# A cached-attention decode kernel on one core: K and V by the slab of a head instead of by quarters, and the softmax cut into pieces

## The chip, the cores and the metric

The kernel runs on one core of a Trainium2 chip. The metric is device time in microseconds (us). Where several runs are compared, all were in the fast state; times are medians, and a ratio is the mean time of one kernel's fast runs over the mean of the other's fast runs of the same rounds, so it is not quite the ratio of the medians quoted. Engines: PE is TensorE (matmuls), DVE is VectorE, ACT is ScalarE, POOL is GpSimd, SP issues the DMAs.

## The reference, cut to what matters

```python
# B=8 sequences, one new token each; 32 query heads share 8 K/V heads; 8192 cached positions of 128
h = layernorm(x) * (1 + ca) + sa
q = h @ wq
scores = einsum(q, k_cache) * 128 ** -0.5
p = softmax(scores);  o = einsum(p, v_cache)
x = x + ga * (o @ wo)
... # a small MLP on x follows
```

K and V together are 268.4 MB, and each byte is used once. Everything else is small.

## The kernel before

The caches are read by units: a quarter of one head's K or V, 512 KB. In each of the 128 partitions a unit is one contiguous run of 16 x 128 bf16 values, 4 KB. The ring has 20 slots, each freed by itself:

```python
def k_units(b): return [("K", b, g, k) for k in range(UPS) for g in range(HKV)]   # UPS = 4, HKV = 8
...
def emit_dma(n):
    s = n % NSLOT                                   # NSLOT = 20
    if n - NSLOT >= 0:
        waits.append(("pe", unit_done[n - NSLOT]))
    step("sp", lambda e: e.dma_start(kv_ring[:, s, :]..., kv_src(u)), waits, ("kv%d" % s, 16))
```

A K unit is transposed on PE, copied out of psA, the PSUM tile that the transposes write, half by DVE (0.69 us for 128x1024) and half by ACT (1.01 us; together the evacuation), then multiplied with the queries (QK). A V unit is multiplied with the probabilities P (PV). PE takes six K units of the next batch ahead (LAG = 6), then K and V by turns. The softmax of a batch runs when its last scores are there:

```python
gq = POOL partition_all_reduce(max)
d2 = cstep("dve", ... tensor_tensor(sview, sview, gb, ALU.subtract), [("gp", gq)])     # 2048 columns
EXP[b] = cstep("act", ... activation(PT_sb, S_sb, ACTF.Exp), w)                        # 2048 columns
...
def emit_sums(b):                                    # before the first PV of b
    sm = mm_group(... ones_h x PT_sb, four matmuls of 512 columns ...)
    RED_done[b] = tensor_reduce;  d_r = reciprocal
    SC_done[b] = cstep("dve", ... tensor_tensor(ptv, ptv, rsb, ALU.mult), ...)         # P scaled, 2048 columns
```

What stood behind such a block in the program of DVE or ACT waited for it: in the prediction's timeline DVE's copies of 179.91 us start as the 2.29 us subtraction of 177.70 us ends, and ACT's of 181.84 us as the 1.91 us exponential of 180.03 us ends, though their transposes were done at 177.2 us.

## Time and profile before

| | before |
|---|---|
| time, median of 15 runs | 756.69 us (753.67 to 758.26) |
| profiled span | 754.0 us |
| PE busy | 76% |
| read from HBM | 283.66 MB |
| plateau of the stream | 407 to 409 GB/s |
| last V unit taken up | 735.2 us |

The busy shares don't tell the bound here; the row of GB/s by slices does (the profile's page cuts the span into 40 equal slices), and what ended the waits of PE tells why that row has dips. The lines are in the prediction.

### The profile page before, as it was taken

The page shows a single profiled execution, that of the slowest core. Times are in us where ns is not written, and L with a number is a line of the kernel's source. Part 1 is how long each engine was busy: PE and PEld are TensorE (multiplying, and loading weights), DVE is VectorE, ACT ScalarE, POOL GpSimd, SP SyncE. Part 2 cuts the span into 40 slices and gives each one's busy share as a digit, 9 for nine tenths or more (in the row PEclk, how much of TensorE's full clock was granted, in tenths as well). Part 3 has the DMA queues.
Part 4 walks back from the last instruction along what each step waited for, and adds up shares of the span by engine and source line. Part 5 has one row for each costly group of instructions (what it writes and reads, how often), then busy time and mean ns, then how long its engine had stood idle before and what let it go on. Part 6 is the DMA issues. An engine that isn't in the chain of part 4 may idle for free.

```text
span 754.0 us, 27966 instructions
## 1 busy us (share of the span) xinstructions
PE 570.1 (76%) x12812; PEld 553.4 (73%) x12820; DVE 252.9 (34%) x379; ACT 298.4 (40%) x314; POOL 4.6 (1%) x17
## 2 busy tenths in 40 slices
PE   3588578876888859885788867798688857988354
PEld 3588578876788859885788867798588846978254
DVE  0244432323433252233323334332532333323302
ACT  2266534443444344452443433443444423534102
POOL 0000000000000000000000000000000000000000
PEclk9999777785887667696687767866687876877555
DMA  8999999999999999999899998999989998999980
GB/s 347 409 408 402 363 403 407 407 407 408 408 406 407 408 395 365 409 407 408 324 378 406 407 408 283 403 407 407 401 315 409 407 408 314 367 408 408 387 320 2
DMA packets 81444, 285.48 MB, mean 379 GB/s; under 512 B 8344, under 2 KB 14256, under 8 KB 80816
## 3 DMA queue, kind: packets, MB, share of 16 engines
q1 hardware_dynamic: 81328, 283.70, 96.3%
q8 instruction: 102, 1.67, 0.9%
q14 instruction: 14, 0.11, 0.0%
HBM read 283.66 MB, written 0.01 MB: 376 GB/s over the span
## 4 chain that ended last, share of the span: by engine, by line
PE 68%; issue 18%; DVE 7%; DMA 3%; ACT 2%; SPq 0%; POOL 0%; ACTq 0%; DVEq 0%; POOLq 0%
PE psA L256 41%; PE psS L293 13%; PE psO L380 13%; DMA W<-in_A_wq_dram 3%; DVE PT_sb L364 2%; DVE S_sb L341 2%; ACT kt_ring L276 2%; PE psM L150 1%; DVE tmax L333 1%; DVE tmax L325 1%; DVE ssum L360 1%; ACT S_sb L309 1%; POOL gmax L337 0%; DVE rs_all L361 0%; SPq L405 0%
## 5 line engine op out<-in xcount | busy, mean ns | idle before, releaser
L276 ACT COPY kt_ring<-psA 128x1024 bf16<-128x1024 bf16 x256 | 258.2, 1012 | 344.6 <-PE psA L256 344.6
L256 PE MATMUL psA<-ident,kv_ring 128*128 128x128 bf16 x4096 | 365.6, 260 | 35.0 <-issue 24.7
L256 PEld LDWEIGHTS psA<-ident,kv_ring 128*128 128x128 bf16 x4096 | 314.7, 119 | 38.2 <-issue 37.9
L275 DVE COPY kt_ring<-psA 128x1024 bf16<-128x1024 bf16 x256 | 176.2, 691 | 404.6 <-PE psA L256 404.5
L293 PE MATMUL psS<-qT_sb,kt_ring 128*128 128x4 bf16 x4096 | 147.3, 166 | 59.8 <-ACT kt_ring L276 40.9
L293 PEld LDWEIGHTS psS<-qT_sb,kt_ring 128*128 128x128 bf16 x4096 | 140.7, 101 | 63.0 <-issue 59.5
L380 PE MATMUL psO<-PT_sb,kv_ring 128*128 128x4 bf16 x4096 | 136.1, 167 | 63.1 <-issue 33.6
L380 PEld LDWEIGHTS psO<-PT_sb,kv_ring 128*128 128x128 bf16 x4096 | 121.6, 100 | 70.6 <-issue 69.4
L345 ACT ACTIVATE PT_sb<-S_sb 128x2048 bf16<-128x2048 f32 x8 | 15.3, 1909 | 38.4 <-DVE S_sb L341 38.4
L309 ACT COPY S_sb<-psS 128x512 f32<-128x512 f32 x32 | 18.9, 592 | 5.5 <-PE psS L293 5.5
L341 DVE TENSOR_TENSOR S_sb<-S_sb,gmax 128x2048 f32<-128x2048 f32 x8 | 18.3, 2292 | 4.5 <-POOL gmax L337 4.5
L364 DVE TENSOR_TENSOR PT_sb<-PT_sb,rs_all 128x2048 bf16<-128x2048 bf16 x8 | 18.3, 2292 | 0.3
L325 DVE TENSOR_TENSOR tmax<-tmax,S_sb 128x512 f32<-128x512 f32 x16 | 11.1, 692 | 20.7 <-ACT S_sb L309 20.7
L150 PE MATMUL psM<-PT_sb,ones_h 128*128 128x512 bf16 x24 | 7.1, 410 | 8.5 <-ACT PT_sb L345 7.9
L494 ACT CAST oT_sb<-psO 128x256 bf16<-128x256 f32 x1 | 0.4, 372 | 28.4 <-PE psO L380 28.4
L150 PEld LDWEIGHTS psM<-PT_sb,ones_h 128*128 128x128 bf16 x32 | 2.6, 100 | 9.8 <-ACT PT_sb L345 7.6
L501 DVE TENSOR_TENSOR tC<-psS,modT 128x32 f32<-128x32 f32 x1 | 0.2, 191 | 27.0 <-PE psS L150 27.0
L150 PE MATMUL psM<-hT_bf,W 128*128 128x8 bf16 x128 | 3.6, 168 | 6.3 <-DMA W<-in_A_wq_dram 6.3
L360 DVE TENSOR_REDUCE ssum<-psM 128x32 f32<-128x512 f32 x8 | 5.5, 692 | 8.2 <-PE psM L150 8.2
L150 PEld LDWEIGHTS psM<-hT_bf,W 128*128 128x128 bf16 x128 | 3.5, 104 | 6.4 <-issue 6.4
L322 DVE TENSOR_TENSOR tmax<-S_sb 128x512 f32<-128x512 f32 x8 | 5.5, 692 | 7.3 <-ACT S_sb L309 7.3
L333 DVE TENSOR_TENSOR tmax<-tmax 128x256 f32<-128x256 f32 (+2 forms) x24 | 7.5, 314 | 0.8
(69 smaller groups left out, 49.7 us busy)
## 6 DMA issues: line engine op xcount, KB each, us to landing
kv_ring<-in_A_k_cache_dram SPq DMA_DIRECT2D x256, 512.0 KB, 13.0
kv_ring<-in_A_v_cache_dram SPq DMA_DIRECT2D x256, 512.0 KB, 12.5
W<-in_A_wq_dram SPq DMA_DIRECT2D x4, 1024.0 KB, 17.3
W<-in_A_wo_dram SPq DMA_DIRECT2D x1, 4096.0 KB, 25.2
W<-in_B_w_dram SPq DMA_DIRECT2D x2, 1792.0 KB, 22.6
W<-in_w_mod_dram SPq DMA_DIRECT2D x1, 3072.0 KB, 11.9
x_sb<-in_A_x_dram SPq DMA_DIRECT2D x1, 8.0 KB
c_sb<-in_c_dram SPq DMA_DIRECT2D x1, 8.0 KB
```

The source lines that it names most:

```text
L150: lambda e, o_=o_, l_=l_, r_=r_, i=i: e.matmul(o_, lhsT=l_, rhs=r_, start=(i == 0), stop=(i == n - 1)),
L256: lambda e, tl=tl: e.transpose(psA_bf[:, base + tl * P: base + (tl + 1) * P], kv_ring[:, slot, tl * DH:(tl + 1) * DH], ident[:, :],),
L275: dv = cstep("dve", lambda e: e.tensor_copy(kt_ring[:, ks, 0: 8 * P], psA_bf[:, base: base + 8 * P]), w)
L276: av = cstep("act", lambda e: e.copy(kt_ring[:, ks, 8 * P: 16 * P], psA_bf[:, base + 8 * P: base + 16 * P]), w)
L293: lambda e, tl=tl: e.matmul(psS[:, half + tl * HQ + REP * g: half + tl * HQ + REP * (g + 1)], lhsT=kt_ring[:, ks, tl * P:(tl + 1) * P], rh ...
L309: sv = cstep("act", lambda e: e.copy(S_sb[:, b % 2, k * 512:(k + 1) * 512], psS[:, half: half + 512]), w)
L325: RUNMAX[b] = cstep("dve", lambda e: e.tensor_tensor(tm, tm, Q, ALU.max), [("dve", RUNMAX[b]), ("act", sv)])
L333: d = cstep("dve", lambda e, hlf=hlf: e.tensor_tensor(tm[:, 0:hlf], tm[:, 0:hlf], tm[:, hlf:2 * hlf], ALU.max), [("dve", d)])
L341: d2 = cstep("dve", lambda e: e.tensor_tensor(sview, sview, gb, ALU.subtract), [("gp", gq)])
L345: EXP[b] = cstep("act", lambda e: e.activation(PT_sb[:, par, :], S_sb[:, par, :], ACTF.Exp), w)
L364: SC_done[b] = cstep("dve", lambda e: e.tensor_tensor(ptv, ptv, rsb, ALU.mult), [("dve", d_r)])
L380: lambda e, tl=tl, t=t: e.matmul(o_cols, lhsT=kv_ring[:, slot, tl * DH:(tl + 1) * DH], rhs=PT_sb[:, par, t * HQ + REP * g: t * HQ + REP * ...
```

## The change

It is meant to stream K and V in longer contiguous pieces and to keep the softmax out of the way of PE. (1) One transfer is a whole head's K or V, 2 MB, 16 KB in each partition; the ring has the same 10 MB as five slab slots, and a slot is refilled when its last unit is done. For that, K goes by head. (2) Subtraction and exponential are cut into four pieces each, placed one or two at a time behind the evacuations of the next batch's K units. (3) P is no longer scaled: a DVE reduction and one small matmul give the sums among the late V units, and the reciprocals multiply the output at the very end. (4) PE takes eight K units ahead instead of six.

```diff
-    NSLOT = 20
+    NSS = 5
+    NSLOT = NSS * UPS
-    LAG = 6
+    LAG = 8
...
-            return [("K", b, g, k) for k in range(UPS) for g in range(HKV)]
+            return [("K", b, g, k) for g in range(HKV) for k in range(UPS)]
...
+            if key not in slab_slot:            # key = (K or V, b, g)
+                if ss_hist[ss]:
+                    prev = ss_hist[ss][-1]
+                    waits.append(("pe", max(unit_done[m] for m in slab_units[prev])))
+                step("sp", lambda e: e.dma_start(kv_ring[:, ss * UPS:(ss + 1) * UPS, :]..., slab_src(*key)), waits, ("kv%d" % ss, 16))
...
-            d2 = cstep("dve", lambda e: e.tensor_tensor(sview, sview, gb, ALU.subtract), [("gp", gq)])
-            EXP[b] = cstep("act", lambda e: e.activation(PT_sb[:, par, :], S_sb[:, par, :], ACTF.Exp), w)
+            for j in range(NPH):
+                todo.append(lambda j=j: emit_sub(b, j))     # 512 columns
+                todo.append(lambda j=j: emit_exp(b, j))     # 512 columns
...
-            SC_done[b] = cstep("dve", lambda e: e.tensor_tensor(ptv, ptv, rsb, ALU.mult), [("dve", d_r)])
...
+                if g == HKV - 2 and k == 0:
+                    emit_reduce(b)
+                if g == HKV - 1 and k == 0:
+                    emit_sums(b)
...
-        d_oT = cstep("act", lambda e: e.copy(oT_sb[:, :], psO[:, 0:B * HQ]), [("pe", PVL)])
+        d_oT = cstep("dve", lambda e: e.tensor_tensor(oT_sb[:, :], psO[:, 0:B * HQ], rs_all[:, :], ALU.mult), ...)
```

## The prediction

> **What bounds the kernel now.** I read the page's slices first, then the busy time by stretch, then the waits, then the timeline around one batch boundary. The slices:
>
> ```profile
> PE   3588578876888859885788867798688857988354
> DMA  8999999999999999999899998999989998999980
> GB/s 347 409 408 402 363 403 407 407 407 408 408 406 407 408 395 365 409 407 408 324 378 406 407 408 283 403 407 407 401 315 409 407 408 314 367 408 408 387 320 2
> HBM read 283.66 MB, written 0.01 MB: 376 GB/s over the span
> ```
>
> The reader is to see a plateau of 407 to 409 GB/s that most slices reach and none of these passes, with dips that come back once per batch (slices 14-15, 19-20, 24-25, 28-29, 33-34, 37-38 counted from 0) and a last slice without traffic. So the kernel is a stream from HBM, with holes.
>
> I check that by a balance. K and V are 512 transfers of 512 KB, 268.4 MB: at 408 GB/s 657.9 us. The modulation and query weights, 7.34 MB, at 426 (below): 17.2 us. The late weights, 7.86 MB: 19.3 us at 408, plus 2.4 us for the low slices 3 and 4 in which they run, 21.7. Instruction fetch (queue q8, 1.67 MB in part 3 of the page): 4.1. The start before the first full rate: 3.5. Sum 704.4 us. The dips: the shortfalls from 408 in the twelve slices named add up to 644 GB/s, times 18.85 us a slice, over 408: 29.8 us. Together 734.2; in the timeline the last V unit is taken up at 735.2. The remaining 18.8 us to 754.0 are the output projection and the MLP. The balance closes within 1 us, so there are three terms to change: rate, dips, tail.
>
> Stretches (length, then busy of PE, its weight loads, DVE, ACT, POOL, then granted clock, DMA share, GB/s):
>
> ```profile
> 6.00:18.00 12.00, 6.66 (x136) 6.34 (x136) 0.45 (x3) 1.03 (x4) 0.59 (x3) 1.00 1.02 426
> 200.00:260.00 60.00, 53.65 (x1253) 52.89 (x1252) 17.99 (x26) 25.75 (x27) 0.00 (x0) 0.76 1.03 407
> 364.00:381.00 17.00, 13.29 (x265) 12.56 (x264) 7.35 (x9) 6.26 (x8) 0.00 (x0) 0.70 0.85 288
> ```
>
> At the same DMA share the first stretch moves 426, not 407. It carries the modulation weights (rows of 6 KB in a partition) and query weights (8 KB); the others carry K and V in pieces of 4 KB. The third is a dip: here the DMA share itself falls, the queue has nothing to do.
>
> Why it runs dry is in the timeline of the boundary at 177 us and in the waits:
>
> ```profile
> 177.70 2.29 DVE L341 TENSOR_TENSOR S_sb<-S_sb,gmax 128x2048 f32<-128x2048 f32 x1 [0.57 <-POOL gmax L337]
> 179.91 1.28 DVE L275 COPY kt_ring<-psA 128x1024 bf16<-128x1024 bf16 x2
> 180.03 1.91 ACT L345 ACTIVATE PT_sb<-S_sb 128x2048 bf16<-128x2048 f32 x1 [4.96 <-DVE S_sb L341]
> 181.84 1.91 ACT L276 COPY kt_ring<-psA 128x1024 bf16<-128x1024 bf16 x2
> 182.98 0.57 PE L293 MATMUL psS<-qT_sb,kt_ring 128*128 128x4 bf16 x16 [5.81 <-ACT kt_ring L276]
> 193.00 2.29 DVE L364 TENSOR_TENSOR PT_sb<-PT_sb,rs_all 128x2048 bf16<-128x2048 bf16 x1
> 195.44 0.56 PE L380 MATMUL psO<-PT_sb,kv_ring 128*128 128x4 bf16 x16 [3.59 <-DVE PT_sb L364]
> ...
> PE psS L293 <- ACT kt_ring L276: 40.9, 9, 6.3
> PE psO L380 <- DVE PT_sb L364: 28.7, 8, 3.6
> ```
>
> PE stops twice per batch. First two evacuations of transposed K queue behind the whole subtraction and the whole exponential (5.8 us of PE idle), then the first PV waits for sum, reciprocal and scaling of P (3.6 us). The six K units between run partly at the half clock. No slot comes free in PE's stops, the SP queue cannot refill, and some 10 us later the DMA queue is empty.
>
> [...] 512 KB transfers reach 408 when many are queued; [...] the copies at 179.91 and 181.84 stand behind softmax work. [...] 16 transposes take 1.87 us at a granted 0.50 and 1.05 us at 1.00.
>
> **The change part by part.** *Slabs.* 512 transfers of 512 KB become 128 of 2 MB; a partition's piece grows from 4 to 16 KB, contiguous over the whole slab. Ring size stays 10 MB. From 426 at 6 to 8 KB, [...] I choose 425 GB/s: 268.4 / 0.425 = 631.6 us, against 657.9: **26 us saved**. The price: a slot is returned only with the last of its four units. I followed the slots by hand: PE holds a K and a V slab, three others (15 us of stream) are queued or landed. At a boundary V6, V7, K0', K1' pass one by one; each reuse finds its slot freed at least 5 us before its turn even if K0' takes 8.5 us at the half clock (4 × 2.13). So I see no stall from the grain itself.
>
> *Softmax cut in pieces.* Out: one subtraction of 2.29 us and one exponential of 1.91 in a block. In: four subtractions of 512 columns (about 0.69 each, as the 128x512 maximum) and four exponentials (about 0.59, as the 128x512 copy), one or two after each K unit, behind that unit's evacuation. The maximum is folded in every phase: six small DVE operations, 0.43 + 0.29 + 0.23 + 0.19 + 0.18 + 0.17 = 1.5 us, 32 times, 48 us of DVE against 26 removed; DVE is busy 34% of the span, and this falls in its idle time. The 5.8 us stop should shrink to under 1.
>
> *Scaling moved to the end.* Out: 2.29 us of scaling, 0.69 + 0.35 of reduce and reciprocal and four matmuls of 0.41 us from the path to PV. In: one DVE reduction of 2048 columns per batch (estimate 2.3 us, by the 2048-column subtraction) and one tiny matmul, placed among V units, when no evacuation is due. With eight K units instead of six before the first V and exponentials ready by the sixth, the 3.6 us stop goes. At the last batch, which has no K to hide behind, the gap of 13.6 us (699.4 to 713.0 in the timeline) becomes about 7, under a full ring.
>
> So PE gets back some 8 × 9 us, but only what reached DMA counts: **the 29.8 us of dips fall to an assumed 4**.
>
> *Tail.* The last PV waits for a whole slab, then does four units at 0.43 us: 1.3 us more.
>
> Sum: 3.5 + 17.2 + 21.7 + 4.1 + 631.6 = 678.1; + 4 dips + 18.8 + 1.3 = 702.2 us of span. The measured median is 2.8 us above the profiled span before; so 705 us.
>
> **The rivals.** *The rate stays at 408* (pieces of 16 KB are cut up again, or 426 came from an idle core and not from row length). For it: that stretch also has little PE work. Against: at 260 to 275 us PE idles too and the stream stays at 405 to 412. Then 26 us are lost again: about 731, still 3% faster.
>
> *PE becomes the bound.* A K and V pair costs PE 2.56 us at half clock and 1.69 at full; the stream delivers one every 2.57 us now and 2.47 then. All at half clock would be 30.4 + 32 × 2.13 + 7 × 32 × 2.56 + 32 × 0.43 + 18.8 = 705 us, no worse than the sum above. But chance stretches of half clock against a ring that frees in lumps could add 5 to 20 us: 710 to 725.
>
> *The grain eats the gain* (the slot waits leave the queue dry between pairs). For it: SP already waits hundreds of us for slots. Against: three slabs ahead. If 1 us were lost at each of the 64 pairs of slabs: 770, slower or the same.
>
> *Only one of the two gains comes*, rate or dips: each is worth 26 us, so about 731 either way.
>
> **Range and chances.** The main sum gives 705. [...] Half of the rate's gain and 10 us of dips: 724. So 690 to 728. Faster by over 2% means below 741.7, which needs the grain to cost or PE to trip before it fails: 0.95. Same 0.04, slower 0.01.
>
> **What would show it.** In the profile of after: plateau slices near 425 (408: the rate step is wrong); no dips at batch boundaries (dips with a falling DMA share: PE or grain); a PV wait for ACT's exponential near zero; QK's wait for ACT's copies far below 40.9 us; about 20 us from the last landing to the end; 16-KB packets, so that the packet count falls from 81444 to about 32000. It is wrong if PE is busy over 90% in every slice while GB/s sags, or if SP's slot waits end in an empty DMA queue.

## The result

The changed kernel took 715.02 us (median of 8 runs, 712.45 to 716.25). The ratio to before is 0.9449, 95% interval 0.9432 to 0.9466: faster by 5.5%. It lies in the range of 690 to 728 (the lower end was my own estimate, which no run shows), 10 us above the 705 of the sum.

The slices of the profiled execution of after:

```profile
span 712.7 us, 27729 instructions
PE   2597858797898888887989887897888888886444
DMA  8999999999999999999999999999999999999960
GB/s 342 427 427 378 335 394 424 425 426 423 426 422 425 424 425 400 414 422 429 424 412 404 425 425 410 409 415 426 426 424 422 425 418 405 406 428 422 428 278 2
DMA packets 26146, 285.44 MB, mean 401 GB/s; under 512 B 2200, under 2 KB 8112, under 8 KB 9136
```

The plateau is 424 to 426 now. The deep dips once per batch are gone; what is left is shallow, apart from slices 3 to 5 and the end. The packet count went from 81444 to 26146, not to my 32000: I had forgotten the packets under 512 B. Their count fell from 8344 to 2200, by 6144, which is 16 for each of the 384 transfers that are no longer there.

PE's waits in after (what waited, for what, us in total, times, longest):

```profile
PE psO L412 <- DMA kv_ring<-in_A_v_cache_dram: 36.5, 21, 7.3
PE psO L412 <- ACT PT_sb L374: 6.2, 1, 6.2
PE psS L315 <- ACT kt_ring L294: 1.4, 1, 1.4
PE psS L315 <- DVE kt_ring L293: 11.1, 15, 1.4
```

QK's wait for ACT's copies fell from 40.9 to 1.4 us. Its wait for DVE's copies rose from 2.4 to 11.1, but in 15 short ones, the longest of 1.4 us. No PV waits for DVE any more. PV waits once for the exponential, at the last batch, 6.2 us. Now PE waits for V to land.

The timeline at the boundary that answers to the one shown of before:

```profile
178.70 0.69 DVE L367 TENSOR_TENSOR S_sb<-S_sb,gmax 128x512 f32<-128x512 f32 x1
179.31 0.68 DVE L293 COPY kt_ring<-psA 128x1024 bf16<-128x1024 bf16 x1
179.91 0.68 DVE L367 TENSOR_TENSOR S_sb<-S_sb,gmax 128x512 f32<-128x512 f32 x1
180.13 0.63 ACT L374 ACTIVATE PT_sb<-S_sb 128x512 bf16<-128x512 f32 x1
180.66 1.00 ACT L294 COPY kt_ring<-psA 128x1024 bf16<-128x1024 bf16 x1
...
187.80 0.54 PE L412 MATMUL psO<-PT_sb,kv_ring 128*128 128x4 bf16 x16
```

Copies and softmax pieces alternate on both engines, and the first PV at 187.80 starts without a wait.

Where the 10 us above the sum are. The last slab is taken up at 692.6 us, the sum had 682.1; after that the tail is 20.1 us, as predicted. Against 425 GB/s the row of GB/s falls short in three places. From 60 to 100 us it is 7.1 us short; the late weights take 7.86 MB / 425 = 18.5 us besides, 25.6 in all where the sum had 21.7: +3.9. Slices 15 to 34 lose about 6.6 us, where I had assumed 4: +2.6. The last slice with traffic loses 3.9, for which I had nothing. Together 10.4. Four stretches show the first and the last of these (length, busy of PE, weight loads, DVE, ACT, POOL, then granted clock, DMA share, GB/s):

```profile
64.00:68.00 4.00, 3.44 (x57) 3.28 (x56) 0.95 (x2) 1.27 (x2) 0.00 (x0) 0.50 0.72 238
72.00:76.00 4.00, 4.00 (x101) 3.97 (x99) 1.96 (x4) 3.38 (x5) 0.00 (x0) 1.00 0.67 201
...
684.00:688.00 4.00, 0.98 (x37) 0.90 (x35) 0.00 (x0) 0.00 (x0) 0.00 (x0) 0.50 0.83 348
688.00:692.00 4.00, 1.94 (x57) 1.80 (x54) 0.36 (x1) 0.00 (x0) 0.00 (x0) 0.50 0.34 143
```

At 64 and 72 us the DMA share falls while PE is busy: the stream waits for PE to free a slab (from 55 to 80 us SP's waits for PE's transposes make 21.3 us). Before the last landing the share falls with nothing left to issue: in windows of 1 us, from 0.68 at 686 us to 0.12 at 691 us. What lowers it is not shown; the profile has only the mean of the 16 DMA engines.

### The profile page after: what moved, and what is told of

The parts are those of the page before. It is cut to its first block, busy times and chain, and to the rows that moved or that the text cites. A ratio compares the mean times of both kernels' runs of the same rounds, so it can differ in the third digit from the quotient of the medians.

```text
span 712.7 us, 27729 instructions
## 1 busy us (share of the span) xinstructions
PE 561.2 (79%) x12804; PEld 544.4 (76%) x12804; DVE 279.5 (39%) x532; ACT 299.0 (42%) x337; POOL 4.6 (1%) x17
## 2 busy tenths in 40 slices
DMA packets 26146, 285.44 MB, mean 401 GB/s; under 512 B 2200, under 2 KB 8112, under 8 KB 9136
## 4 chain that ended last, share of the span: by engine, by line
PE 46%; DMA 34%; issue 13%; DVE 4%; ACT 2%; SPq 1%; POOL 0%; POOLq 0%; ACTq 0%
PE psA L274 29%; DMA kv_ring<-in_A_v_cache_dram 19%; DMA kv_ring<-in_A_k_cache_dram 12%; PE psS L315 9%; PE psO L412 7%; DMA W<-in_A_wq_dram 3%; DVE tmax L344 1%; DVE kt_ring L293 1%; ACT S_sb L331 1%; ACT kt_ring L294 1%; DVE tmax L339 1%; PE psM L155 1%; DVE ssum L384 1%; SPq L437 0%; DVE colmax L344 0%
## 5 line engine op out<-in xcount | busy, mean ns | idle before, releaser
L274 PE MATMUL psA<-ident,kv_ring 128*128 128x128 bf16 x4096 | 352.6, 254 | 36.4 <-issue 19.5
L274 PEld LDWEIGHTS psA<-ident,kv_ring 128*128 128x128 bf16 x4096 | 303.7, 116 | 38.7 <-issue 22.2
L384 DVE TENSOR_REDUCE ssum<-PT_sb 128x32 f32<-128x2048 bf16 x8 | 30.3, 3792 | 0.7 <-ACT PT_sb L374 0.7
L344 DVE TENSOR_TENSOR tmax<-tmax 128x128 f32<-128x128 f32 (+3 forms) x128 | 28.3, 221 | 4.4
L339 DVE TENSOR_TENSOR tmax<-S_sb 128x256 f32<-128x256 f32 x32 | 13.6, 426 | 30.3 <-ACT S_sb L331 30.3
L367 DVE TENSOR_TENSOR S_sb<-S_sb,gmax 128x512 f32<-128x512 f32 x32 | 21.7, 684 | 0.6 <-POOL gmax L348 0.6
L374 ACT ACTIVATE PT_sb<-S_sb 128x512 bf16<-128x512 f32 x32 | 20.4, 641 | 3.1 <-DVE S_sb L367 3.1
L155 PE MATMUL psM<-ssum,ones_f 128*128 128x32 f32 x16 | 5.0, 408 | 6.6 <-DVE ssum L384 6.5
L155 PEld LDWEIGHTS psM<-ssum,ones_f 128*128 128x128 f32 x16 | 4.0, 311 | 7.0 <-DVE ssum L384 6.9
L348 POOL PARTITION_ALL_REDUCE gmax<-colmax x8 | 3.5, 436 | 647.3 <-DVE colmax L344 647.3
## 6 DMA issues: line engine op xcount, KB each, us to landing
W<-in_A_wq_dram SPq DMA_DIRECT2D x4, 1024.0 KB, 20.1
W<-in_B_w_dram SPq DMA_DIRECT2D x2, 1792.0 KB, 20.1
```

What stands on the lines that cost most here:

```text
L155: lambda e, o_=o_, l_=l_, r_=r_, i=i: e.matmul(o_, lhsT=l_, rhs=r_, start=(i == 0), stop=(i == n - 1)),
L274: lambda e, tl=tl: e.transpose(psA_bf[:, base + tl * P: base + (tl + 1) * P], kv_ring[:, slot, tl * DH:(tl + 1) * DH], ident[:, :],),
L339: d = cstep("dve", lambda e: e.tensor_tensor(tm[:, 0:256], Q[:, 0:256], Q[:, 256:512], ALU.max), [("act", sv)])
L344: d = cstep("dve", lambda e, hlf=hlf, dst=dst: e.tensor_tensor(dst, tm[:, 0:hlf], tm[:, hlf:2 * hlf], ALU.max), [("dve", d)])
L367: SUBD[b, j] = cstep("dve", lambda e: e.tensor_tensor(sv, sv, gb, ALU.subtract), [("gp", gqs[b])])
L374: v = cstep("act", lambda e: e.activation(PT_sb[:, par, j * 512:(j + 1) * 512], S_sb[:, par, j * 512:(j + 1) * 512], ACTF.Exp), w)
```

## The experiments

My theory had two independent gains, piece length and softmax, and a coarse grain that costs nothing. Every run below gave a correct result. Each is compared with the kernel before in the same rounds (three rounds). The changed kernel's own 715.02 and 0.9449 are from rounds of their own.

### Same 2 MB transfers, pieces of 4 KB

```diff
-            return cache[b, g].rearrange("(p t) d -> p (t d)", p=P)
+            return cache[b, g].rearrange("(p s t) d -> p s (t d)", p=P, s=UPS)
...
-                    kv_ring[:, ss * UPS:(ss + 1) * UPS, :].rearrange("p s f -> p (s f)"), slab_src(*key)),
+                    kv_ring[:, ss:NSLOT:NSS, :], slab_src(*key)),
...
-            return ss * UPS + k, "kv%d" % ss, val
+            return k * NSS + ss, "kv%d" % ss, val
```

> The changed kernel, with the four units of a slab placed apart in the ring, so that the same 2 MB transfer (same waits, same order, 128 of them) is written in pieces of 4 KB instead of 16 KB. Theory (the length of the contiguous piece sets the plateau): plateau back at 407 to 409 GB/s, packet count up from 26146 to about 75000, time 715 + 24 = about 739 us (733 to 745). Rival (fewer and larger transfers raise the rate, not longer pieces): plateau stays near 425, 713 to 718 us.

Measured: 737.42 us, ratio 0.9776 (0.9753 to 0.9799), 75298 packets.

### The softmax half alone: 512 KB units, 20 slots

The transfer function of before is put back, with 20 semaphores; everything else stays as in the changed kernel.

```diff
...
-                    waits.append(("pe", max(unit_done[m] for m in slab_units[prev])))
...
+            if n - NSLOT >= 0:
+                waits.append(("pe", unit_done[n - NSLOT]))
...
```

> The changed kernel with the transfers of before: 512 KB each, 20 slots freed one by one, 4-KB pieces; unit order, softmax in pieces and final scaling stay. It is the softmax half of the change alone. Theory: no dips at batch boundaries, plateau 408, so 757 less some 20 to 26 us of dips: 731 to 737 us. Beside the run with 2 MB transfers in 4-KB pieces it tells what the coarse grain costs: if the grain costs some 6 to 8 us, this run is that much faster than that one; if the grain is free, the two agree within 2 us.

Measured: 735.86 us, ratio 0.9754 (0.9729 to 0.9778).

The rows of GB/s, first of the run with 4-KB pieces in 2 MB transfers:

```profile
GB/s 330 413 408 393 343 389 408 408 407 408 408 407 407 408 407 397 408 390 409 408 393 406 406 408 394 401 409 407 406 384 406 407 409 390 407 403 403 408 278 2
```

and of the run with 512 KB units:

```profile
GB/s 343 410 409 406 365 396 407 408 408 408 408 407 408 409 408 407 407 407 408 402 401 407 400 408 408 400 401 406 404 402 408 393 408 408 399 405 408 402 262 2
```

Both have the old plateau of 408, so here the length of the piece sets it (408 GB/s at 4 KB, 425 at 16 KB), not the size or the number of the transfers. In the first run the 16 KB of a partition still lie together in HBM and only their places in the ring are apart; so the piece that counted here is contiguous on both sides: 75298 packets against 26146, at the same 2 MB a transfer. And the two runs are 1.6 us apart: with the new softmax the grain costs next to nothing by itself. The piece length is worth 737.4 - 715.0 = 22 us, the softmax half, with the order and the lead that belong to it, 755.5 - 735.9 = 20 us.

### The slab half alone: the softmax of before on slabs

```diff
-            for j in range(NPH):
-                todo.append(lambda j=j: emit_sub(b, j))
-                todo.append(lambda j=j: emit_exp(b, j))
+            d2 = cstep("dve", lambda e: e.tensor_tensor(sv4, sv4, gb4, ALU.subtract), [("gp", gq)])    # 2048 columns
+            EXP[b] = cstep("act", lambda e: e.activation(PT_sb[:, par, :], S_sb[:, par, :], ACTF.Exp), w)
...
+            SC_done[b] = cstep("dve", lambda e: e.tensor_tensor(ptv, ptv, rsb, ALU.mult), [("dve", RS_done[b])])
...
-                waits.append(("act", EXP[b]))
+                waits.append(("dve", SC_done[b]))
```

> The changed kernel with the softmax of before put back: one subtraction and one exponential over 2048 columns, sums by matmuls over P, and P scaled before the first PV; slabs, order of units and the lead of 8 K units stay. It is the slab half alone. Theory (the stops of PE cost the stream some 20 us even with slabs, and the longer pieces alone bring 26): 733 to 741 us, plateau 425 with dips once per batch. Rival (the lead of 8 K units or the slabs alone hide the chain): 715 to 720 us.

Measured: 764.93 us, ratio 1.0158 (1.0104 to 1.0211): 1 to 2% slower than before, which at the mark of 2% is unclear. Both theories failed: the longer pieces were there and nothing came of them. One of its four runs is a stray (772.69; the others 763.85 to 765.28). Its rows by slices:

```profile
DMA  8998999999599995999869995999969998799970
GB/s 349 427 425 326 372 407 403 421 425 425 246 400 424 426 416 226 427 425 427 364 273 427 424 425 236 410 420 426 405 240 426 422 428 348 286 425 425 421 323 3
```

The plateau is 425, but once per batch the stream falls to 226 to 286, deeper than before. The timeline of the DMA issues around the first hole, then two stretches of it:

```profile
188.03 0.33 SPq L244 DMA_DIRECT2D kv_ring<-in_A_v_cache_dram  x1
194.19 0.33 SPq L244 DMA_DIRECT2D kv_ring<-in_A_k_cache_dram  x1
209.57 0.33 SPq L244 DMA_DIRECT2D kv_ring<-in_A_v_cache_dram  x1
```

```profile
200.00:206.00 6.00, 3.88 (x73) 3.91 (x74) 2.67 (x2) 1.01 (x1) 0.00 (x0) 0.57 0.34 145
206.00:212.00 6.00, 6.00 (x127) 6.00 (x125) 1.70 (x3) 2.34 (x3) 0.00 (x0) 0.58 0.26 63
```

With the lead over at 194 us, PE waits 5.3 us for the scaled P. Then it works on a K and a V slab by turns, partly at the half clock (granted 0.57 and 0.58 in the two stretches), and neither is finished before 209.6. For 15.4 us no slot comes free, about what three slabs ahead hold at 4.9 us each. With single units the first slot of the pair would come free after one unit, as I read the code.

### Both halves undone, the new order kept

The run above, with the transfers of the softmax half:

```diff
...
-                    waits.append(("pe", max(unit_done[m] for m in slab_units[prev])))
...
+            if n - NSLOT >= 0:
+                waits.append(("pe", unit_done[n - NSLOT]))
...
```

> The changed kernel with both halves undone, slabs and softmax, while the order of units (by head group) and the lead of 8 K units stay. Why was the slab half alone 765 us and not 737? Theory now (a stop of PE costs more when slots come back only with whole slabs, because after the lead nothing is freed until a K and a V slab are both worked off): with slots freed one by one the time falls back to that of before, 752 to 762 us, although the pieces are 4 KB again. Rival (the new order, the lead of 8 or the sums of this layout, which stand behind the phase maximum, cost by themselves): well above, 770 to 790 us.

Measured: 763.03 us, ratio 1.0099 (1.0075 to 1.0123). A little above my 762, so neither expectation holds whole: 7 us of it are not the grain. In this order PV's wait for the scaled P is 40.7 us in 8 times, against 28.7 in before, since a phase maximum stands in DVE's queue ahead of the sums. That is 12 us more of stops; that they make the 7 us is my reading, not tested apart. The wait of before and that of this run:

```profile
PE psO L380 <- DVE PT_sb L364: 28.7, 8, 3.6
PE psO L421 <- DVE PT_sb L403: 40.7, 8, 5.4
```

The table of the four, medians in us (the changed kernel's is from other rounds):

| | softmax of before | softmax in pieces |
|---|---|---|
| 512 KB units, 20 slots | 763.0 | 735.9 |
| 2 MB slabs, 5 slots | 764.9 | 715.0 |

Slabs bring 21 us beside the new softmax and nothing beside the old one. The softmax brings 27 us on units and 50 on slabs. So the gains aren't independent: the longer pieces pay only where PE has no stops.

### One stop at a time, on slabs

Subtraction and exponential in a block, scaling at the end as in the changed kernel:

```diff
-                todo.append(lambda j=j: emit_sub(b, j))
-                todo.append(lambda j=j: emit_exp(b, j))
...
+            d2 = cstep("dve", lambda e: e.tensor_tensor(sv4, sv4, gb4, ALU.subtract), [("gp", gq)])
...
+            EXP[b] = cstep("act", lambda e: e.activation(PT_sb[:, par, :], S_sb[:, par, :], ACTF.Exp), w)
```

> The changed kernel with one subtraction and one exponential of 2048 columns in a block again; final scaling and slabs stay. It puts back only the first stop of PE (5 to 6 us per batch). Theory: a stop of 5 to 6 us with a ring freed by slabs costs part of the 50 us that both stops cost: 722 to 738 us. Rival (only the second stop, at the first PV, matters, as it delays the release of both slabs of a pair): 714 to 718 us.

Measured: 738.06 us, ratio 0.9761 (0.9714 to 0.9808), its runs spread from 732.74 to 741.14: faster than before, but the interval leaves open whether by 2%. QK waits for ACT's copies again:

```profile
PE psS L315 <- ACT kt_ring L294: 40.1, 8, 6.5
```

Pieces stay, P is scaled before the first PV:

```diff
...
+            SC_done[b] = cstep("dve", lambda e: e.tensor_tensor(ptv, ptv, rsb, ALU.mult), [("dve", RS_done[b])])
...
-                waits.append(("act", EXP[b]))
+                waits.append(("dve", SC_done[b]))
```

> The changed kernel with sums, reciprocal and scaling of P before the first PV again; subtraction and exponential stay in pieces. It puts back only the second stop of PE (3.6 to 5.3 us per batch). Theory: 722 to 742 us; if the two stops add, this excess over 715 and that of the block run make about 50 us together; if the ring absorbs one stop and not two, both stay below 728 us. Rival (only the first stop matters): 714 to 718 us.

Measured: 734.25 us, ratio 0.9728 (0.9703 to 0.9753), its five runs from 727.97 (the profiled one) to 736.05. PV waits for the scaled P again:

```profile
PE psO L422 <- DVE PT_sb L404: 38.4, 8, 5.4
```

Each stop, some 5 us per batch, costs 19 to 23 us alone, 42 together; both at once cost 50. With runs that spread over 8 us in both, they add as far as these can tell, and neither rival holds. The block run came out at the upper edge of what I expected.

### The holes at 64 to 76 us: late weights earlier, or one more slot

```diff
-        LATE_LOAD_AT = 2 * NSLOT
+        LATE_LOAD_AT = 28
```

> The changed kernel with the late weight loads (7.86 MB) issued at unit 28, right after the last K slab of the first batch, instead of at unit 40. Theory (two holes between 64 and 76 us, in which GB/s falls to 238 and 201, come from slot waits while PE is still in the first K phase, and the weights need no slot): the holes close, 3 to 5 us less, about 711 us. Rival (the low rate from 60 to 100 us is all due to the weights' own short rows): 715 us, within 1 us.

Measured: 711.14 us, ratio 0.9430 (0.9404 to 0.9455), span 709.5. Between 60 and 72 us it moves 349 to 353 GB/s at a DMA share of 1.04 and more: the hole is filled with the weights, at the rate of their short rows (1 and 3.5 KB, 48 and 145 ns a packet by the medians of the changed kernel's trace).

```diff
-    NSS = 5
+    NSS = 6
...
-    NKT = 4
+    NKT = 3
...
-        tmax = sbt("tmax", [P, 2, 512], F32)
+        tmax = sbt("tmax", [P, 2, 256], F32)
...
-        LATE_LOAD_AT = 2 * NSLOT
+        LATE_LOAD_AT = 40
```

> The changed kernel with six slab slots instead of five, 12 MB of ring; for room the ring of transposed K has three slots instead of four and the scratch of the maximum 256 columns instead of 512. Theory (the remaining dips of 400 to 415 GB/s and the holes at 64 to 76 us are slot waits of the coarse grain): both nearly go, 706 to 711 us. Rival (the small dips are the memory's or the engines' own): 714 to 716 us.

Measured: 711.25 us, ratio 0.9413 (0.9394 to 0.9432). Just above the expected range. From 110 to 650 us it moves 421 GB/s against 420 in the changed kernel: the sixth slot closes the early holes, not the shallow dips later on. Both at once, with the edits of six slots and

```diff
-        LATE_LOAD_AT = 40
+        LATE_LOAD_AT = 28
```

> Six slab slots and the late weights issued at unit 28, both together. If both only close the same holes between 64 and 76 us, they don't add: 710 to 712 us. If six slots close the later dips and the earlier weights the first holes, they add: 705 to 708 us.

Measured: 711.03 us, ratio 0.9406 (0.9370 to 0.9442). They don't add, so they close the same holes: slot waits in the first K phase. All three medians lie below the lowest of the changed kernel's 8 runs (712.45); but they were not run in the same rounds, and the intervals of the ratios touch or overlap. About 4 us, likely and not proved. This combination has the lowest median measured, within 0.3 us of the other two, and it beats before by 5.9%.

### Half slabs: 1 MB in pieces of 8 KB

```diff
-    NSS = 5
+    NSS = 10
+    SPU = 2
...
-            key = u[:3]
+            key = u[:3] + (u[3] // SPU,)
```

> The changed kernel with half slabs: 1 MB transfers in pieces of 8 KB, ten slots of two units each, the same 10 MB. Theory: the plateau at 8 KB lies close to that at 16 KB (420 to 425 GB/s), and the finer grain gives back the small dips and part of the holes at 64 to 76 us: 710 to 716 us. Rival (the rate grows in proportion with the piece, so that 8 KB gives half of the gain, 416): 720 to 727 us.

Measured: 719.14 us, ratio 0.9512 (0.9482 to 0.9542). I missed by 3 us: the plateau is 419, lower than I thought, and the time lies just under the rival's range. With twelve half slabs and the late weights at unit 28, room made as for six slabs:

```diff
-    NSS = 10
+    NSS = 12
...
-        LATE_LOAD_AT = 2 * NSLOT
+        LATE_LOAD_AT = 28
```

> A version that should beat all: twelve half slabs of 1 MB in 8-KB pieces (12 MB of ring), late weights at unit 28. Theory: plateau about 424, no holes, last half slab instead of last slab before the final PV, 1 us less at the end: 704 to 710 us. If 8 KB costs rate: 714 to 722 us.

Measured: 719.32 us, ratio 0.9515 (0.9484 to 0.9545). The theory missed and the second branch came true: 8 KB costs rate, and nothing was gained over ten half slabs. The row of GB/s of that run:

```profile
GB/s 344 420 419 371 398 419 419 419 418 418 418 418 419 419 420 417 418 419 420 418 419 419 419 420 418 419 418 420 418 418 420 418 418 416 417 418 418 387 171 2
```

This is the even stream that I had wished for, at 416 to 420, and it is slower than the uneven one at 425. The grain left little to win: even from 110 to 650 us is 419, and the changed kernel with its shallow dips moves 420.

### A lead of six K units instead of eight

```diff
-    LAG = 8
+    LAG = 6
```

> The changed kernel with a lead of 6 K units before the first V unit, as before, instead of 8. The pieces of softmax are issued after the second to the sixth K unit of the next batch, so the last exponential comes just before the first PV. Theory (the lead matters little once softmax is in pieces): 715 to 719 us, the first PV waits at most 1 us for the exponential. Rival (the lead is what hides the chain): 722 to 735 us.

Measured: 714.60 us, ratio 0.9453 (0.9421 to 0.9485), as the changed kernel. The lead doesn't matter once the softmax is in pieces.

## Why the prediction was right, point by point

- *The bound and the balance.* Right. A stream with holes: the time follows the holes and the plateau together. One example was ill chosen: the boundary shown at 177 us has PE's two stops and no dip after them (406 to 410 GB/s from 172 to 232 us, in windows of 6 us). The first dip follows the next boundary, 308 GB/s from 280 to 286. So a stop of PE empties the DMA queue after some boundaries and not after others.
- *Slabs, 26 us saved.* The size was right: 22 us measured between equal transfers with 4-KB and 16-KB pieces, with 425 against 408 on the plateau. The way to it was partly luck. I took 426 from the stretch that loads the weights and read it as the rate of 6 to 8 KB pieces; the step from there to 425 was my estimate. K and V in 8-KB pieces reached only 419. The same weights, in the same pieces, moved 426 GB/s between 6 and 18 us in before and 415 in the changed kernel. So 426 was one draw of a stretch that scatters, and not the rate of a piece; 425 came true because the pieces are 16 KB.
- *"So I see no stall from the grain itself."* Right at the boundaries for the whole change (1.6 us between slabs and units of equal pieces). It failed in the first K phase, which I had not followed: there the two holes cost about 4 us, and a sixth slot or earlier weights close them. And the clause hid a condition: with the old softmax the grain takes the whole gain of the longer pieces. As far as the trace of that run shows, in that combination my rival "the grain eats the gain" was right.
- *Softmax in pieces, scaling at the end.* Right: both stops are gone, and each was worth some 20 us on slabs. The longest wait of a QK for a copy is 1.4 us, where I had said under 1, and the gap at the last batch is 6.2 us, where I had said 7. The pieces took 0.68 and 0.64 us, close to 0.69 and 0.59. The reduction took 3.79 us, not the estimated 2.3; at its place among V units that showed only as 6.5 us of PE waiting for it in four batches, under a stream that went on.
- *"The 29.8 us of dips fall to an assumed 4".* The term that was too small. Left were 6.6 us of shallow dips and 3.9 at the end. The end was there before as well, inside the 29.8: the slice with the last landing has 320 GB/s, and from 731.0 to 735.2 us it moved 66 GB/s. No softmax could take it away, and I should have left it in.
- *Late weights, 21.7 us.* Measured 25.6, by the holes just named.
- *Tail, 1.3 us more.* Right: 20.1 us from the last landing to the end.
- *The half clock rival.* It did not become the bound: PE was busy 79% of the span, and a granted clock of 0.762 was enough.

What stays open: why the shallow dips remain with six slots, and why the DMA share falls before the last landing. That the coarse grain takes the longer pieces' gain beside the old softmax is read from one trace; 2 MB transfers in 4-KB pieces beside the old softmax, which would show it apart, were not run.

## What to carry to other kernels

Balance a streaming kernel by bytes, rate, holes and tail before changing it, and leave the end of the stream in its own term. Longer contiguous pieces raised the plateau here (408 GB/s at 4 KB, 419 at 8 KB, 425 at 16 KB), but a coarser buffer made the holes after the consumer's stops deeper (slices down to 226 GB/s, against 283 in before); remove the stops first, then coarsen. Test such halves in a square of four, since each alone can mislead: here one half alone gained nothing.

## What the runs showed of the hardware

- The rate of K and V depended on the contiguous piece: 408 GB/s at 4 KB (in 512 KB and in 2 MB transfers alike), 419 at 8 KB, 425 at 16 KB. One piece of K or V took 160 ns at 4 KB and 611 ns at 16 KB (medians of the packets in the traces of before and of the changed kernel). As an estimate from these two, that is 150 ns for each 4 KB plus 10 ns for the piece; for 8 KB it gives 310 ns, and the packets of the query weights, of 8 KB, took 312 and 309 ns in the two traces.
- One core alone held 425 GB/s from HBM: the plateau of the changed kernel is 424 to 426 in the slices.
- In the changed kernel PE was busy 9.49 of the 10 us from 350 to 360 us at a granted 0.50, and 4.00 of the 4 us from 72 to 76 us at a granted 1.00. No run tells what set the granted clock.
- The end of the transfers: in the last 8 us before the last landing the DMA share fell to 0.83 and then 0.34, some 4 us of the stream. The profile doesn't show why.
